# Attention and expert kernel on one Trainium2 core: other zero products in the head, six row buffers blanked later, whole sketches for the last queries, a new written order

## The chip, the core and the metric

The kernel runs on one core of a Trainium2 chip. A core has five engines that run their own instruction streams side by side and wait for one another by semaphores: TensorE (PE in the profile; its weight loads are PEld), VectorE (DVE), ScalarE (ACT), GpSimd (POOL) and SyncE (SP), which only issues transfers. The metric is the time of one execution on the device, in microseconds, as the median of the runs. The profile shows one execution; its times count from the first instruction of the span.

## The reference

```python
def phi(x):
    a = np.einsum('rd,bhsd->bhsr', S1, x)
    b = np.einsum('rd,bhsd->bhsr', S2, x)
    return np.einsum('bhsi,bhsj->bhsij', a, b).reshape(*x.shape[:-1], r * r)
q_p, k_p = (phi(q), phi(k))
kv = np.einsum('bhsf,bhsd->bhfd', k_p, v)
z = np.sum(k_p, axis=2)
num = np.einsum('bhsf,bhfd->bhsd', q_p, kv)
den = np.einsum('bhsf,bhf->bhs', q_p, z)[..., None] + 1e-06
attn = num / den                       # (4, 4, 1088, 32) -> x: 4352 rows of 128
...
e_idx = np.argmax(x @ w_gate, axis=1)  # 8 experts
...
for e in range(E):
    h = np.maximum(x[mask] @ w1[e], 0.0)          # 128 -> 1024
    out[mask] = gate_w[mask, None] * eom[mask, e, None] * (h @ w2[e])
```

Everything is in 32-bit floats. The attention is linear: keys and queries are turned into 64 products each ("sketches"), the keys' products are summed with the values for each of 4 batches, and each query's products are multiplied by these sums. Then each of the 4352 rows goes through the one expert of eight that its logits choose.

## The kernel before, in words

The program is a set of named steps, each bound to one engine, and `ORDER` is a written list of their names. The steps are emitted in that order, and every engine keeps its own steps in it. A step whose input is not there holds up all that stands behind it on its engine. The number of a step is a group of 512 rows (0 to 8; group 8 has 256), a batch (0 to 3) or a tile of 128 rows.

Attention, by groups. `Lk.g`, `Lq.g`, `Lv.g` (SP) load keys, queries and values into rings of 4, 3 and 4 buffers. `Sk.g`/`Sq.g` (PE) make the sketches, in one of two forms: a group listed in `QUARTERS` takes products of 64x64 (L400) into the ring `w`, any other takes products of 128x128, called whole (L406), into the ring `t`. Both rings lie in PSUM and have two buffers. `B` (ACT, L424) copies one half of the sketch, `M` (DVE, L429) adds the other half to it and gives the PSUM buffer back, `P` (DVE, L437) multiplies out. `A g.b` (PE, L466) sums keys times values of batch b; `C`, `KV` (ACT) copy the sums out, `GT`, `GC`, `GM`, `GK` make the gate's columns of them. `T g` (PE, L515) turns a group of query products, `TC` (ACT) copies it, `N g` (PE, L532) multiplies it by the sums, `R` (ACT, L545) copies the outcome, `X` (DVE, L557 to L562) makes the logits.

Routing, in three routes of three groups. When a route's last `X` is done, `CA`, `CB` (DVE), `PL` (PE), `WE`, `LA`, `SL`, `HP`, `HT` (DVE) give each row its place; `ST` (SP) stores the rows to DRAM (`xt`); `ID` (PE, L646) and `IA`, `IX` (DVE, L651 to L661) make the lists of row numbers.

Experts, by tiles of 128 rows. `F t` (POOL, L802) gathers a tile's rows from `xt` by the list, `XD` (DVE, L812) divides, `TN` (PE, L816) turns, `TC.t` (DVE, L822) copies, `UP` (PE, L829), `RL`, `DN` (PE, L843) and `Y` are the expert's two layers, `O` (POOL, L942) scatters the rows into the output. The first list serves tiles 0 to 7 and needs `IX0` and `ST0`; tiles 0 to 15 go alone, later tiles in groups of three (L881 to L922). `W e a` (ACT's queue, L228) loads half of an expert's weights, 512 KB.

Head. Before anything is loaded, PE runs products of zeros (`zeros`, L167): `WARM` of them at first, and one and two behind the two small products that turn the sketch matrices (`turn_rows`, L318). ACT blanks the sums' buffers and all 12 row buffers `xin` (`blank`, L369) before its first `B`.

Of the kernel before, what the change touches and what calls it, by code (L numbers as in the profile page):

```python
# [34 lines left out]
ORDER = """
Lk.0 Lk.1 Lk.2 Lk.3 Sk.0 Bk.0 Mk.0 Pk.0 Lq.0 Lq.1 Lv.0 Lv.1 Lv.2 Lq.2 Sk.1 Bk.1 Sk.2 Sq.1 A0.0 Sq.0 Bq.1 Bk.2 Mk.1 Pk.1 Mq.1 Mk.2 Pk.2 Bq.0 A1.0 A2.0
Lk.4 Lq.3 LG Lq.4 Sq.2 Bq.2 Lk.5 Lv.3 Lk.6 Lq.5 Lv.4 Sk.3 Mq.0 Pq.1 Pq.0 Mq.2 KV0 Bk.3 C0 WG Mk.3 Pk.3 T1 Sq.4 GT0 T0 Bq.4 GC0 Sk.4 Mq.4 Pq.4 GM0 CF0
A2.1 CC0 TC0 Bk.4 W00 GK0 N0 Mk.4 Pk.4 Pq.2 A3.1 A4.1 Sq.3 TC1 R0 C1 GT1 GC1 Bq.3 X0 KV1 T2 Sk.6 Mq.3 Pq.3 GM1 N1 Lq.6 Lk.7 Lv.5 Lv.6 Lk.8 CF1 TC2 W01
Bk.6 W10 GK1 Mk.6 Pk.6 N2 R1 R2 A4.2 Sq.5 Sk.5 T4 T3 X1 X2 CA0 Bk.5 Bq.5 Mq.5 TC4 CB0 Mk.5 Pk.5 TC3 Sk.7 Sq.6 Bq.6 CE0 N3 PL0 Bk.7 R3 Mq.6 WE0 LA0 SL0
HP0 HT0 Lv.7 Lv.8 Lq.7 Lq.8 ST0 A5.2 A6.2 C2 GT2 KV2 GC2 GM2 Sq.7 GK2 N4 R4 Pq.5 ID0 CF2 IA0 IX0 Mk.7 Pk.7 LC F0 F1 F2 A6.3 Sk.8 T5 Bk.8 Bq.7 Mk.8  # L40
Pk.8 CN0 A7.3 A8.3 TC5 Sq.8 W11 Bq.8 C3 Mq.7 Pq.7 N5 XD0 Mq.8 CT0 TN0 T7 TC.0 XD1 GT3 TN1 R5 TC7 W20 W21 GC3 X3 TC.1 X4 XD2 Pq.8 UP0 UP1 RL0 W30 W31
W40 RL1 TN2 DN0 GM3 T8 Y0 W41 CC1 GK3 KV3 TC8 DN1 X5 CA1 TC.2 CB1 PL1 CN1 F3 F4 F5 F6 O0 XD3 Pq.6 F7 CE1 CT1 CF3 KD N8 N7 TN3 R8 UP2 Y1 R7 W50 W51 RL2
W60 XD5 TC.3 XD4 WE1 LA1 SL1 HP1 TN4 UP3 RL3 TN5 TC.5 XD6 T6 TC.4 HT1 DN2 TC6 TN6 N6 R6 ST1 ID1 UP4 DN3 TC.6 IA1 IX1 X6 XD7 X7 X8 CA2 W61 RL4 CC2 CB2
W70 Y2 UP5 DN4 TN7 TC.7 UP6 Y3 RL5 W71 O1 O2 O3 F8 F9 F10 F11 F12 Y4 RL6 CN2 PL2 SL2 XD8 DN5 UP7 TN8 CE2 WE2 HP2 TC.8 XD9 LA2 HT2 DN6 TN9 TC.9 XD11
XD10 EN RL7 Y5 Y6 UP8 RL8 TN11 TN10 DN7 Y7 DN8 Y8 UP9 TC.10 UP10 TA XD12 O4 F13 TC.11 XD13 FT1 ID2 RL9 ST2 FW45 FW41 FW43 DN9 Y9 ZY TN12 O5 F14 IA2
IX2 O6 F15 F16 O7 F17 TC.12 UP11 RL10 DN10 Y10 RL11 DN11 Y11 TN13 UP12 F18 F19 F20 O8 F21 O9 F22 O10 F23 XD15 TC.13 XD14 UP13 TN14 RL12 TN15 DN12
TC.14 UP14 RL13 FT0 XG0 TC.15 DN13 FT2 NG0 UP15 RL14 Y12 Y13 DN14 Y14 XG1 RL15 DN15 Y15 CG0 O11 F24 O12 F25 O13 F26 O14 F27 FW44 FW42 FW40 NG1 UA0
RG0.0 RG0.1 CG1 UB0 RG0.2 RG0.3 XG2 O15 F28 F29 F30 DG0 UA1 YC0 RG1.0 RG1.1 BG0 NG2 CG2 YG0 UB1 RG1.2 RG1.3 F31 O16 F32 O17 F33 O18 XG3 DG1 UA2 YC1
RG2.0 RG2.1 BG1 NG3 CG3 YG1 UB2 RG2.2 RG2.3 F34 O19 F35 O20 F36 O21 XG4 DG2 UA3 YC2 RG3.0 RG3.1 BG2 NG4 CG4 YG2 UB3 RG3.2 RG3.3 F37 O22 F38 O23 F39
O24 XG5 DG3 UA4 YC3 RG4.0 RG4.1 BG3 NG5 NT CG5 FI FX YG3 UB4 RG4.2 RG4.3 F40 O25 F41 O26 F42 O27 XG6 DG4 UA5 YC4 RG5.0 RG5.1 BG4 NG6 CG6 YG4 UB5 RG5.2  # L50
RG5.3 F43 O28 F44 O29 O30 DR30 XG7 DG5 UA6 YC5 RG6.0 RG6.1 BG5 NG7 CG7 YG5 UB6 RG6.2 RG6.3 O31 O32 O33 XD40 XD41 DG6 UA7 YC6 RG7.0 RG7.1 BG6 TN40
TC.40 YG6 XD42 EX UB7 RG7.2 RG7.3 O34 O35 O36 DG7 YC7 TN41 TC.41 TN42 TC.42
""".split()
# [27 lines left out]
def kernel(  # L81
# [1116 lines left out]
```

## Time and profile before

| | |
|---|---|
| runs | 198.92 us median of 3 (198.47 to 199.83) |
| profiled execution | 198.53 us, span 196.5 us (2.0 us lie around the span) |
| TensorE busy | 188.5 us, 96% of the span |
| VectorE / ScalarE / GpSimd busy | 114.1 / 73.0 / 91.0 us |
| mean granted clock of TensorE | 0.977 |

Busy TensorE means that a product is under way, at whichever of its two clocks (1.2 and 2.4 GHz). Whether it could go faster has to be read from the length of equal groups at different places, and from what stands just before a gap.

### The profile page before, as it was taken

To read this page: it belongs to the slowest core of one execution; us is meant where nothing else is said; L and a number is where in the kernel's file an instruction comes from. 1 tells how busy PE (TensorE), PEld (TensorE's weight loads), DVE (VectorE), ACT (ScalarE), POOL (GpSimd) and SP (SyncE) were. 2 spreads that over 40 slices of the span, in tenths; PEclk is the share of its full clock that TensorE was granted. 3 is DMA by queue.
4 is the path that set the end of the run, shared out by engine and by line. 5 is a ranking of instruction groups with operands and counts; after the bars stand their busy time and mean duration, and the time that the engine had idled before them with its cause. 6 is when DMAs were issued, how large, how long until landed. Compare 5 with 4: busy or idle time off the path is not lost.

```text
span 196.5 us, 5598 instructions
## 1 busy us (share of the span) xinstructions
PE 188.5 (96%) x2209; PEld 170.6 (87%) x2209; DVE 114.1 (58%) x296; ACT 73.0 (37%) x173; POOL 91.0 (46%) x119
## 2 busy tenths in 40 slices
PE   7999989889999999999999999999999999999990
PEld 6999989789999999999999997777998876698990
DVE  5589869998686967568452842342633616065120
ACT  7526776643567634333022314030332221123210
POOL 1840000007726005787047877757677376235172
PEclk9999999966999999999999999999999999999997
DMA  5969965161699799456999422122112020000011
GB/s 167 344 189 314 278 240 176 59 196 46 211 326 343 219 344 292 152 177 180 414 420 403 169 59 64 52 56 63 51 30 63 3 65 14 18 17 30 27 32 30
DMA packets 14878, 31.11 MB, mean 158 GB/s; under 512 B 2553, under 2 KB 7815, under 8 KB 14064
## 3 DMA queue, kind: packets, MB, share of 16 engines
q1 hardware_dynamic: 9328, 16.44, 24.4%
q10 hardware_dynamic: 2320, 8.39, 12.7%
q0 software_dynamic: 3184, 5.65, 9.6%
q8 instruction: 31, 0.51, 1.1%
q14 instruction: 15, 0.12, 0.2%
HBM read 25.53 MB, written 5.90 MB: 160 GB/s over the span
## 4 chain that ended last, share of the span: by engine, by line
PE 46%; DMA 36%; issue 7%; POOL 5%; DVE 1%; ACT 1%; POOLq 1%; DVEq 0%; ACTq 0%
DMA xin<-xt,putf 14%; DMA out_dram<-ys,putf 14%; PE w L829 12%; DMA xin<-xt,putfar 8%; PE y L843 7%; PE t L406 6%; PE acc L843 5%; PE w L532 4%; PE acc L466 4%; POOL xin L802 3%; PE w L515 3%; POOL out_dram L942 2%; PE w L400 2%; PE t L646 1%; PE t L816 1%
## 5 line engine op out<-in xcount | busy, mean ns | idle before, releaser
L802 POOL DMA_INDIRECT xin<-xt,putf x36 | 40.7, 1131 | 50.4 <-DVE ab L429 32.6
L942 POOL DMA_INDIRECT out_dram<-ys,putf x36 | 36.2, 1006 | 41.7 <-ACT ys L846 12.1
L895 PE MATMUL w<-vt,wt 128*128 128x256 f32 (+5 forms) x128 | 32.3, 396 | 0.0
L829 PE MATMUL w<-xsT,wt 128*128 128x128 f32 x256 | 30.8, 276 | 0.0
L829 PEld LDWEIGHTS w<-xsT,wt 128*128 128x128 f32 x256 | 29.7, 192 | 0.1
L895 PEld LDWEIGHTS w<-vt,wt 128*128 128x128 f32 x128 | 22.7, 190 | 6.0 <-DVE kT L901 0.4
L901 DVE TENSOR_SCALAR kT<-w 128x768 f32<-128x768 f32 x8 | 7.7, 957 | 32.9 <-PE w L895 32.9
L834 ACT ACTIVATE hT<-w 128x1024 f32<-128x1024 f32 x13 | 13.3, 1023 | 19.6 <-PE w L829 19.6
L843 PE MATMUL y<-wt,hT 128*128 128x128 f32 x144 | 17.7, 276 | 0.0
L843 PEld LDWEIGHTS y<-wt,hT 128*128 128x128 f32 x144 | 16.8, 192 | 0.1
L912 PE MATMUL acc<-kT,wt 128*128 128x256 f32 (+5 forms) x64 | 16.2, 396 | 0.1
L912 PE MATMUL acc<-qT,wt 128*128 128x256 f32 (+5 forms) x64 | 16.0, 392 | 0.0
L916 ACT COPY kT<-acc 128x384 f32<-128x384 f32 x8 | 3.8, 478 | 30.9 <-PE acc L912 30.9
L912 PEld LDWEIGHTS acc<-kT,wt 128*128 128x128 f32 x64 | 11.7, 190 | 3.6 <-issue 0.6
L912 PEld LDWEIGHTS acc<-qT,wt 128*128 128x128 f32 x64 | 11.8, 190 | 2.9
L843 PE MATMUL acc<-wt,hT 128*128 128x128 f32 x112 | 13.7, 275 | 0.0
L843 PEld LDWEIGHTS acc<-wt,hT 128*128 128x128 f32 x112 | 13.1, 192 | 0.0
L903 ACT ACTIVATE qT<-w 128x768 f32<-128x768 f32 x8 | 6.5, 810 | 13.9 <-PE w L895 13.9
L466 PE MATMUL acc<-vt,kp 128*64 128x33 f32 (+1 forms) x288 | 11.2, 230 | 0.0
L532 PE MATMUL w<-kz,qpT 64*64 64x49 f32 x544 | 10.6, 227 | 0.5 <-issue 0.5
L437 DVE TENSOR_TENSOR kp<-ab 128x1024 f32<-128x1024 f32 (+1 forms) x9 | 10.5, 1166 | 0.7 <-PE acc L466 0.3
L466 PEld LDWEIGHTS acc<-vt,kp 128*64 128x64 f32 (+1 forms) x288 | 10.1, 144 | 0.7
(184 smaller groups left out, 297.3 us busy)
## 6 DMA issues: line engine op xcount, KB each, us to landing
wt<-in_w_dram ACTq DMA_DIRECT2D x16, 512.0 KB, 6.0
xall<-in_w_dram SPq DMA_DIRECT2D x3, 1024.0 KB, 9.9
xt<-xall SPq DMA_DIRECT2D x2, 1176.0 KB, 6.5
vt<-in_v_dram SPq DMA_DIRECT2D x8, 260.0 KB, 5.3
kT<-in_k_dram SPq DMA_DIRECT2D x8, 256.0 KB, 3.9
qT<-in_q_dram SPq DMA_DIRECT2D x8, 256.0 KB, 3.8
qp<-in_w_dram SPq DMA_DIRECT2D x1, 1024.0 KB
qpT<-in_w_dram SPq DMA_DIRECT2D x1, 1024.0 KB, 14.2
```

What stands on the lines that cost most here:

```text
L406: nc.tensor.matmul(ps[:, j].rearrange("p i x -> p (i x)"), src[:, j * 128:(j + 1) * 128], Sb.rearrange("p i h x -> p (i h x)"), start=True ...
L437: nc.vector.tensor_mul(res[:, :n], bview(av, [list(av.ap[1]), list(av.ap[2]), [0, r]]), bview(bv, [list(bv.ap[1]), [0, r], list(bv.ap[2])]))
L466: nc.tensor.matmul(now["acc", b][64 * h:64 * (h + 1), s], kp[p0:p0 + n, heads_at("k", g, j, s) + h].rearrange("s i j -> s (i j)"), now["v" ...
L532: nc.tensor.matmul(ps[64 * t:64 * (t + 1), h, 2 * j + s], now["qT", g][64 * h:64 * (h + 1), 2 * j + s, 64 * t:64 * (t + 1)], kz[(c * 128 + ...
L802: nc.gpsimd.indirect_dma_start(out=xin[room(t)], out_offset=None, in_=xt[:n, :], in_offset=bass.IndirectOffsetOnAxis(ap=index(t), axis=0), ...
L829: nc.tensor.matmul(ps[:, c], w[:, c], x[:, own(t)], start=True, stop=True)
L834: nc.scalar.activation(out, now["h", t], ACTF.Relu)
L843: nc.tensor.matmul(ps, h[:, c], w[:, c], start=(c == 0), stop=(c == FC - 1))
L895: nc.tensor.matmul(now["h", "g", e, s][:, c, :n], w[:, s * (FC // 4) + c], x[:, :n], start=True, stop=True)
L901: nc.vector.tensor_scalar_max(wide_h[s], src, 0.0)
L912: nc.tensor.matmul(ps[:, :n], w[:, c], wide_h[c // (FC // 4)][:, c % (FC // 4), :n], start=(c == 0), stop=(c == FC - 1))
L942: apart("out", nc.gpsimd.indirect_dma_start(out=out, out_offset=bass.IndirectOffsetOnAxis(ap=index(t), axis=0), in_=at_ys(t), in_offset=No ...
```

## The change

Four things. The zeros of the head become one product of 512 columns and one of 256 (before, five of 128), then one of 128 behind the first turned matrix (before, one of 64) and one of 192 behind the second (before, two of 48). Six of the 12 row buffers are blanked in two new steps of ScalarE, `BX0` and `BX1`, which stand in the order behind `Bk.1` and behind `R2`. The query groups 6, 7 and 8 leave `QUARTERS`, so that their sketches are whole. And the written order is a new one, up to the start of the grouped tiles; from there on it is the old one.

```diff
-WARM = 5
+WARM = (4, 2)
-QUARTERS = {("k", 0), ("q", 0), ("k", 1), ("q", 6), ("q", 7), ("q", 8)}
+QUARTERS = {("k", 0), ("q", 0), ("k", 1)}
 ORDER = """
-Lk.0 Lk.1 Lk.2 Lk.3 Sk.0 Bk.0 Mk.0 Pk.0 Lq.0 Lq.1 Lv.0 Lv.1 Lv.2 Lq.2 Sk.1 Bk.1 Sk.2 Sq.1 A0.0 Sq.0 Bq.1 Bk.2 Mk.1 Pk.1 Mq.1 Mk.2 Pk.2 Bq.0 A1.0 A2.0
+Lk.0 Lk.1 Lk.2 Lq.0 Lq.1 LG Lv.0 Lv.1 Sk.0 Bk.0 Mk.0 Pk.0 Lk.3 Lk.4 Lq.2 Sk.2 Sk.1 Sq.0 Bk.2 Bk.1 BX0 A0.0 Mk.2 Pk.2 Mk.1 Pk.1 Sq.1 Bq.1 Bq.0 Sq.2
...
-    def zeros(n, w=128):
-        for i in range(n):
-            nc.tensor.matmul(warm[:, 0, :w], idle, idle[:, :w], start=True, stop=True)
-    zeros(WARM)
+    def zeros(n, k, w):
+        for _ in range(n):
+            nc.tensor.matmul(warm[:, 0, :k * w].rearrange("p (k x) -> p k x", x=w), idle, bview(idle, [[0, k], [1, w]]), start=True, stop=True)
+    for k in WARM:
+        zeros(1, k, DM)
...
-        zeros(1 + i, 64 - 16 * i)
+        zeros(1, 1 + i, 128 - 32 * i)
...
-    for t in xin:
+    at_first = len(xin) - 6
+    for t in xin[:at_first]:
         blank(t, 2, W // 2)
+
+    def blank_rows(i):
+        for t in xin[at_first + 3 * i:at_first + 3 * (i + 1)]:
+            blank(t, 2, W // 2)
...
+    for i in range(2):
+        add(f"BX{i}", "ACT", [], lambda i=i: blank_rows(i))
```

What the new order moves stands in the engines' own rows. First VectorE of the kernel before, from the query products of group 5 to the first tile's division; `rows_of` to `putf` are `IA0` and `IX0`, which finish the first list, and `xdiv` is `XD0`:

```order
L437 TENSOR_TENSOR qp<-ab_226 128x1024
L651 COPY rows_of<-t_64 128x80
L659 TENSOR_TENSOR valf_902<-rows_of 128x8
L660 TENSOR_SCALAR nonef_903<-valf_902 128x8
L661 SCALAR_TENSOR_TENSOR putf_904<-valf_902,nonef_903 128x8
L429 TENSOR_TENSOR ab_225<-t_65,ab_225 128x256
L437 TENSOR_TENSOR kp<-ab_225 128x1024
L429 TENSOR_TENSOR ab_226<-t_64,ab_226 128x128
L437 TENSOR_TENSOR kp<-ab_226 128x512
L429 TENSOR_TENSOR ab_225<-w_66,ab_225 128x256
L437 TENSOR_TENSOR qp<-ab_225 128x1024
L812 TENSOR_TENSOR xdiv_262<-xin 128x128
```

The same stretch of the changed kernel, from the list on, where lines stand six higher:

```order
L657 COPY rows_of<-t_64 128x80
L665 TENSOR_TENSOR valf_927<-rows_of 128x8
L666 TENSOR_SCALAR nonef_928<-valf_927 128x8
L667 SCALAR_TENSOR_TENSOR putf_929<-valf_927,nonef_928 128x8
L443 TENSOR_TENSOR qp<-ab_216 128x1024
L435 TENSOR_TENSOR ab_217<-t_65,ab_217 128x256
L563 RECIPROCAL xall<-xall 128x16
L565 TENSOR_TENSOR lg_225<-xall 128x256
L567 TENSOR_TENSOR lg_225<-lg_225 128x4x32
L568 TENSOR_TENSOR L_227<-lg_225 128x64
L443 TENSOR_TENSOR qp<-ab_217 128x1024
L818 TENSOR_TENSOR xdiv_252<-xin 128x128
```

The key products of groups 7 and 8 (`kp`) stood behind the list and now stand ahead of it; behind it come the queries of groups 7 and 6 and the logits of group 3.

TensorE of the kernel before, from the sketch of query group 8 to the first up products (L829, tiles 0 and 1) and a little behind them:

```order
L400 MATMUL w_67<-Sb,qT 64x64 x8
L532 MATMUL w_66<-kz_207,qpT 64x49 x32
L816 MATMUL t_64<-ident,xdiv_262 128x128
L515 MATMUL w_67<-ident,qp 128x128 x8
L490 MATMUL t_65<-ident,kv_233 64x128
L816 MATMUL t_64<-ident,xdiv_263 128x128
L829 MATMUL w_66<-xsT_260,wt_92 128x128 x8
L829 MATMUL w_67<-xsT_260,wt_94 128x128 x8
L816 MATMUL t_65<-ident,xdiv_262 128x128
L843 MATMUL y_69<-wt_93,hT 128x128 x8
L501 MATMUL t_64<-wgb,kzT_231 64x32 x2
```

The same stretch of the changed kernel:

```order
L412 MATMUL t_64<-Sb,qT 128x128 x2
L521 MATMUL w_67<-ident,qp 128x128 x8
L538 MATMUL w_66<-kz_203,qpT 64x49 x32
L538 MATMUL w_67<-kz_204,qpT 64x49 x32
L698 MATMUL t_65<-cum_240,ones 64x8 x2
L822 MATMUL t_64<-ident,xdiv_252 128x128
L521 MATMUL w_66<-ident,qp 128x128 x8
L822 MATMUL t_64<-ident,xdiv_253 128x128
L835 MATMUL w_67<-xsT_250,wt_89 128x128 x8
L835 MATMUL w_66<-xsT_250,wt_91 128x128 x8
L521 MATMUL w_67<-ident,qp 128x128 x4
L849 MATMUL y_69<-wt_90,hT 128x128 x8
```

`N7` (the second row of 64x49) and `T6` (the second L521) have come ahead of the first up products, and the sketch of query group 8 is two whole products in the place of eight small ones. `GM3` (L501) has moved far ahead as well.

ScalarE of the changed kernel, where the sums of batch 1 are kept (`KV1`, the four rows of `kz`) and query group 3 is copied (`Bq.3`, the row of `ab`):

```order
L513 COPY kz_201<-t_64 64x2x16 x2
L488 COPY kz_202<-acc_68 64x2x32
L489 COPY kz_202<-acc_68 64x2
L488 COPY kz_202<-acc_68 64x2x32
L489 COPY kz_202<-acc_68 64x2
L591 COPY oh_237<-carry 128x8
L430 COPY ab_217<-t_65 128x256
```

In the kernel before `Bq.3` stood ahead of `KV1`; now it stands behind it.

## Rows read from the trace of the kernel before

**Rows 1.** The page: busy time of each engine, and the granted clock in 40 slices.

```profile
PE 188.5 (96%) x2209; PEld 170.6 (87%) x2209; DVE 114.1 (58%) x296; ACT 73.0 (37%) x173; POOL 91.0 (46%) x119
PEclk9999999966999999999999999999999999999997
```

**Rows 2.** Stretches: start:end, length, busy us (instructions) by engine, clock, DMA share, GB/s.

```profile
35.00:40.00 5.00, 3.92 (x155) 3.40 (x147) 4.76 (x13) 3.48 (x15) 0.00 (x0) 1.00 0.32 100
40.00:45.00 5.00, 5.00 (x138) 4.66 (x139) 4.57 (x10) 1.53 (x5) 0.03 (x1) 0.58 0.48 147
45.00:50.00 5.00, 5.00 (x121) 4.63 (x123) 3.42 (x7) 1.88 (x5) 4.08 (x4) 0.74 0.33 99
190.00:196.50 6.50, 1.65 (x15) 1.46 (x14) 0.35 (x1) 0.27 (x1) 2.67 (x3) 0.84 0.11 33
```

**Rows 3.** All waits of PE: us in total, times, longest.

```profile
PE w L167 <- DVE maskh L231: 1.1, 1, 1.1
PE t L501 <- ACT kzT L494: 0.6, 1, 0.6
PE w L532 <- issue: 0.5, 1, 0.5
PE t L490 <- ACT kv L476: 0.5, 1, 0.5
```

**Rows 4.** The chain that ended last, 43.9 to 55.9 us: start, us, what.

```profile
43.89 0.18 DVE putf L661
44.97 0.33 POOL xin L802
...
47.07 4.41 DMA xin<-xt,putf
51.50 0.30 DVE xdiv L812
51.85 0.33 PE t L816
52.18 3.72 PE w L829 x32
```

**Rows 5.** Time line of PE: start, us, what. The head, then equal groups at full clock.

```profile
1.14 2.50 PE L167 MATMUL w<-ys 128*128 128x128 f32 x10 [1.14 <-DVE maskh L231]
4.86 1.09 PE L167 MATMUL w<-ys 128*128 128x48 f32 x4
5.88 1.99 PE L400 MATMUL w<-Sb,kT 64*64 64x64 f32 x64
7.79 2.07 PE L406 MATMUL t<-Sb,kT 128*128 128x128 f32 x8
16.70 1.06 PE L406 MATMUL t<-Sb,qT 128*128 128x128 f32 x8
21.82 1.36 PE L466 MATMUL acc<-vt,kp 128*64 128x33 f32 x40
34.67 0.70 PE L400 MATMUL w<-Sb,qT 64*64 64x64 f32 x32
```

**Rows 6.** The same time line: groups at 44 to 71 us.

```profile
45.60 1.91 PE L515 MATMUL w<-ident,qp 128*128 128x128 f32 x8
57.72 0.30 PE L501 MATMUL t<-wgb,kzT 64*64 64x32 f32 x4
60.88 1.87 PE L532 MATMUL w<-kz,qpT 64*64 64x49 f32 x96
66.64 1.04 PE L515 MATMUL w<-ident,qp 128*128 128x128 f32 x8
```

**Rows 7.** Time line of ACT: blanks and the first copies of sketches.

```profile
3.76 3.17 ACT L369 COPY xin<-ys 128x196 f32<-128x196 f32 x12
7.08 0.37 ACT L424 COPY ab<-w 128x256 f32<-128x256 f32 x1 [0.15 <-PE w L400]
10.95 0.65 ACT L424 COPY ab<-t 128x256 f32<-128x256 f32 x2 [2.65 <-PE t L406]
```

**Rows 8.** Waits of DVE from 7 to 45 us.

```profile
DVE ab L429 <- ACT ab L424: 3.6, 4, 2.3
DVE xall L557 <- ACT xall L546: 1.0, 1, 1.0
```

**Rows 9.** Time line of DVE: the key products of groups 7 and 8.

```profile
44.42 1.22 DVE L437 TENSOR_TENSOR kp<-ab 128x1024 f32<-128x1024 f32 x1
46.15 0.29 DVE L429 TENSOR_TENSOR ab<-t,ab 128x128 f32<-128x128 f32 x1 [0.50 <-ACT ab L424]
```

More of the change, by code (lines that the diff above doesn't have):

```diff
@@ L33 @@
 NY = 6
-QUARTERS = {("k", 0), ("q", 0), ("k", 1), ("q", 6), ("q", 7), ("q", 8)}
+QUARTERS = {("k", 0), ("q", 0), ("k", 1)}
 ORDER = """
-Lk.0 Lk.1 Lk.2 Lk.3 Sk.0 Bk.0 Mk.0 Pk.0 Lq.0 Lq.1 Lv.0 Lv.1 Lv.2 Lq.2 Sk.1 Bk.1 Sk.2 Sq.1 A0.0 Sq.0 Bq.1 Bk.2 Mk.1 Pk.1 Mq.1 Mk.2 Pk.2 Bq.0 A1.0 A2.0
-Lk.4 Lq.3 LG Lq.4 Sq.2 Bq.2 Lk.5 Lv.3 Lk.6 Lq.5 Lv.4 Sk.3 Mq.0 Pq.1 Pq.0 Mq.2 KV0 Bk.3 C0 WG Mk.3 Pk.3 T1 Sq.4 GT0 T0 Bq.4 GC0 Sk.4 Mq.4 Pq.4 GM0 CF0
-A2.1 CC0 TC0 Bk.4 W00 GK0 N0 Mk.4 Pk.4 Pq.2 A3.1 A4.1 Sq.3 TC1 R0 C1 GT1 GC1 Bq.3 X0 KV1 T2 Sk.6 Mq.3 Pq.3 GM1 N1 Lq.6 Lk.7 Lv.5 Lv.6 Lk.8 CF1 TC2 W01
@@ L39 @@
[L39 to L50, printed above, removed]
@@ L51 @@
-RG5.3 F43 O28 F44 O29 O30 DR30 XG7 DG5 UA6 YC5 RG6.0 RG6.1 BG5 NG7 CG7 YG5 UB6 RG6.2 RG6.3 O31 O32 O33 XD40 XD41 DG6 UA7 YC6 RG7.0 RG7.1 BG6 TN40
-TC.40 YG6 XD42 EX UB7 RG7.2 RG7.3 O34 O35 O36 DG7 YC7 TN41 TC.41 TN42 TC.42
+Lk.0 Lk.1 Lk.2 Lq.0 Lq.1 LG Lv.0 Lv.1 Sk.0 Bk.0 Mk.0 Pk.0 Lk.3 Lk.4 Lq.2 Sk.2 Sk.1 Sq.0 Bk.2 Bk.1 BX0 A0.0 Mk.2 Pk.2 Mk.1 Pk.1 Sq.1 Bq.1 Bq.0 Sq.2
+Bq.2 Mq.1 Mq.0 Pq.1 Mq.2 Pq.0 A1.0 Lk.5 Lv.2 Lv.3 A2.0 Lq.3 Lv.4 Lk.6 Lq.4 Lq.5 Sk.4 Sk.5 T1 W00 C0 Bk.4 Bk.5 KV0 Mk.4 WG Mk.5 Pk.4 Sk.3 CF0 A2.1 Bk.3
@@ new lines @@
+W01 TC1 Pq.2 Mk.3 Pk.3 T0 GT0 Sq.3 GC0 TC0 W10 GM0 A3.1 A4.1 GK0 N0 KV1 CC0 Bq.3 R0 Sk.6 Bk.6 C1 Pk.5 Mq.3 Pq.3 Mk.6 X0 T2 Sq.4 GT1 Bq.4 GC1 TC2 N1
+GM1 CF1 A4.2 Lk.7 Lv.5 Lv.6 Lq.6 Lq.7 Lk.8 Lv.7 Lv.8 Mq.4 Pq.4 Pk.6 GK1 N2 A5.2 Sk.7 Sk.8 A6.2 W11 R1 R2 BX1 Bk.8 Bk.7 KV2 W20 W21 C2 T4 X1 X2 CA0
+Mk.8 Mk.7 Pk.7 CB0 Sq.5 CF2 A6.3 Bq.5 TC4 CE0 Mq.5 Pk.8 A7.3 GT2 GC2 PL0 A8.3 GM2 C3 GK2 WE0 LA0 SL0 HT0 HP0 T3 GT3 Sq.7 GC3 GM3 TC3 Bq.7 GK3 N4 KV3
+R4 Sq.6 Mq.7 ID0 Pq.5 N3 IA0 IX0 ST0 Lq.8 LC F0 F1 F2 F3 F4 T5 Sq.8 W30 Bq.6 R3 Pq.7 T7 TC5 Bq.8 TC7 W31 N5 R5 Mq.6 X3 Pq.6 XD0 Mq.8 Pq.8 N7 CF3 KD
@@ new lines @@
+CN0 TN0 T6 TC.0 XD1 TN1 CT0 TC.1 R7 CC1 TC6 UP0 UP1 RL0 W40 T8 RL1 DN0 X4 X5 CA1 XD3 XD2 CB1 PL1 SL1 CN1 CT1 N6 CE1 Y0 TC8 W41 N8 R6 W50 W51 TN3 TN2
+DN1 TC.2 TC.3 XD4 UP2 TN4 F5 F6 HT1 XD5 O0 F7 Y1 R8 CC2 RL2 W60 TN5 UP3 WE1 LA1 TC.4 UP4 ST1 X6 DN2 HP1 X7 XD6 TC.5 XD7 X8 CA2 RL3 DN3 TN6 ID1 IA1 IX1
+TC.6 RL4 W61 Y2 W70 Y3 W71 UP5 TN7 CB2 TC.7 CE2 WE2 UP6 CN2 PL2 DN4 RL5 DN5 RL6 Y4 DN6 Y5 Y6 O1 O2 O3 F8 F9 F10 F11 F12 O4 F13 O5 F14 O6 SL2 HP2 HT2
+XD8 TN8 XD9 TC.8 UP7 RL7 EN XD10 TN9 ID2 IA2 XD11 TC.9 LA2 IX2 TA ST2 FW40 UP8 TN10 UP9 TN11 RL8 DN7 Y7 TC.11 TC.10 XD13 RL9 XD12 TN13 DN8 Y8 DN9 Y9
@@ new lines @@
+TN12 TC.12 UP10 RL10 UP11 UP12 XD14 FT2 DN10 Y10 F15 F16 O7 F17 F18 F19 RL11 TC.13 TN14 DN11 Y11 RL12 ZY FT1 UP13 RL13 TC.14 XD15 XG0 DN12 DN13 NG0
+FT0 TN15 TC.15 Y12 UP14 UP15 RL14 Y13 DN14 RL15 DN15 FW42 FW44 F20 O8 CG0 Y14 F21 XG1 O9 Y15 F22 O10 F23 O11 F24 O12 F25 O13 F26 O14 F27 FW45 FW41
+FW43 UA0 RG0.0 NG1 CG1 RG0.1 UB0 RG0.2 RG0.3 XG2 O15 F28 F29 F30 DG0 UA1 YC0 RG1.0 RG1.1 BG0 NG2 CG2 YG0 UB1 RG1.2 RG1.3 F31 O16 F32 O17 F33 O18 XG3
+DG1 UA2 YC1 RG2.0 RG2.1 BG1 NG3 CG3 YG1 UB2 RG2.2 RG2.3 F34 O19 F35 O20 F36 O21 XG4 DG2 UA3 YC2 RG3.0 RG3.1 BG2 NG4 CG4 YG2 UB3 RG3.2 RG3.3 F37 O22
@@ L53 @@
+F38 O23 F39 O24 XG5 DG3 UA4 YC3 RG4.0 RG4.1 BG3 NG5 NT CG5 FI FX YG3 UB4 RG4.2 RG4.3 F40 O25 F41 O26 F42 O27 XG6 DG4 UA5 YC4 RG5.0 RG5.1 BG4 NG6 CG6
+YG4 UB5 RG5.2 RG5.3 F43 O28 F44 O29 O30 DR30 XG7 DG5 UA6 YC5 RG6.0 RG6.1 BG5 NG7 CG7 YG5 UB6 RG6.2 RG6.3 O31 O32 O33 XD40 XD41 DG6 UA7 YC6 RG7.0 RG7.1
+BG6 TN40 TC.40 YG6 XD42 EX UB7 RG7.2 RG7.3 O34 O35 O36 DG7 YC7 TN41 TC.41 TN42 TC.42
 """.split()
```

## The prediction

> **What bounds the kernel now.** I read the page first: TensorE is busy for 188.5 of 196.5 us, no other engine for more than 60% [rows 1]. Its list of waits is short: 1.1 us at the start, and three waits of half a microsecond [rows 3]; the end costs 4.9 us more, since of the last 6.5 us it works in 1.65 [rows 2]. So the time is TensorE's work, and what a change can win is of three kinds: waits, stretches at the lower clock, and work that goes away.
>
> Then the stretches. The granted clock is 0.58 in 40 to 45 us and 0.74 in 45 to 50 [rows 2]. With two levels, 1.2 and 2.4 GHz, a mean of 0.58 is 4.2 us at the lower one and 0.74 is 2.6, together 6.8 us. Just before the fall TensorE had waited for ScalarE twice, 0.5 and 0.6 us [rows 3], and was busy for only 3.92 us of 5 [rows 2]. What it costs shows on equal groups: eight turns take 1.91 us at 45.60 and 1.04 at 66.64 [rows 6]. The head is slow too, though the clock column does not say so: eight whole sketch products take 2.07 us at 7.79 and 1.06 at 16.70 [rows 5].
>
> Last the chain. From 43.9 to 52 us it does not run through TensorE: the first list (`putf`) is ready at 44.07, the first gather starts at 44.97, the second at 47.07 and lands 4.41 us later, `XD1` and `TN1` follow at 51.50 and 51.85, and the up products at 52.05 to 52.18 [rows 4]. So the first up product stands **8.0 us behind the list**, whatever TensorE does meanwhile; the work between is filler. This decides the case: what TensorE loses ahead of 52 us has been paid partly by filler that was there anyway.
>
> **The change part by part.**
>
> *Zeros.* Ten passes of 128 columns took 2.50 us, about 0.22 each [rows 5]. By columns, 512 and 256 take six times 128 in each of two passes, 12 x 0.213 = 2.56 us against 10 x 0.213 = 2.13: 0.4 us more, which makes the first turned matrix about 0.2 us later (PE had a 0.2 us hole there). The last zeros fall from four passes (1.0 us, as long for 48 columns as for 128 [rows 5]) to two of 0.32: 0.4 us less. So the first sketch starts 0.2 us earlier, at about 5.7. The denser head may also bring the full clock before the 8 to 10 us at which it came. That is worth at most 1.0 us in the group at 7.79 [rows 5] and the same again in the small sketches ahead of it (1.99 us for 64 passes against twice 0.5), but VectorE is next there: it needs 1.6 us for every group it adds and multiplies (0.41 + 1.22 [rows 9]) and then has no hole. I take 0.3 us from VectorE's earlier start, with 0 and 1.0 as ends.
>
> The Trainium skill ("TensorE: Matmul & The Clock Gate", section "What's actually happening") says that the number of slow products at the start differs from run to run and that the ramp is less than 1% of a typical span and nothing to fit to. The rows agree with the size: the slow head costs about 2 us of TensorE. By that rule the head would give nothing that can be counted on, a rival below.
>
> *Blanks.* Twelve take 3.17 us, 0.26 each [rows 7]. Six fewer free ScalarE 1.6 us earlier, but its first copy had waited for TensorE already (0.15 us [rows 7]): nothing. `BX0` and `BX1`, 0.8 us each, fall into holes of ScalarE such as the 2.65 us ahead of 10.95 [rows 7]. If a hole is gone, 0.8.
>
> *Whole sketches.* A quartered group of 32 passes takes 0.52 us from start to start (0.70 with its tail), a whole one 0.89 (1.06) [rows 5]: 0.37 more for groups 6 and 7, half as much for group 8, together 0.9 us of TensorE. All three stand ahead of the first up product, where TensorE waits. Cost 0; 0.9 if that cover is gone.
>
> *The order, behind the first up product.* Three pieces have moved from behind it to ahead of it: `N7`, two thirds of 1.87 us = 1.25; `T6`, 0.87 (1.04 less the tail); `GM3`, 0.23 [rows 6]. TensorE works without a wait from there to 191.6 us, so the end comes **2.35 us earlier** if the first up product stays where it is. In the later part, the second list and third list stand at about the same number of tiles or earlier; I find no new wait there, and the grouped tiles are untouched.
>
> *The order, ahead of it.* The first list needs VectorE. It now does the keys of groups 7 and 8 first: 1.6 and 0.9 us [rows 9], so 2.5 us later. Against that go VectorE's waits up to the list: 1.0 for the logits of group 1, and 3.6 for copies less the 2.3 before its first instruction, 1.3 [rows 8], about 0.5 in smaller ones; with the 0.3 of the earlier start, 3.1 less. One wait is new. `Mq.3` needs `Bq.3`, which stands on ScalarE behind `KV1`; `KV1` waits for the sums `A3.1` and `A4.1`, 1.3 us of TensorE [rows 5] that start only when `Pk.3` is done. Behind `Pk.3` VectorE has one product (1.1 us) to do, while sums, tail, keeping (0.55), and the copy (0.37) take 2.7: it waits 1.6 us, with all products of groups 3 to 8, and so the list, behind it. Sum: 2.5 - 3.1 + 1.6 = **1.0 us later**, list at 45.1, first up product at 53.0. Ends: 0.5 earlier (no such wait) and 2.5 later.
>
> *Sum.* 2.35 - 1.0 = 1.35 us. The profiled execution took 198.53, which gives 197.2; the median of the runs is 0.4 above it, which gives 197.6. I forecast 197.4.
>
> The dip at 40 to 50 us adds nothing to this, which is the step most easily got wrong. Its 3.4 us, and the two waits ahead of it, were filler time: without them TensorE runs out of filler earlier. Before, it arrived at `TN1` with about 0.1 us to spare. Now it saves 3.4 us of dip, 1.6 of waits and some of the head, about 6, gets 2.35 + 0.9 us more to do, and so waits about 2 us in front of `TN1` and another 1 to 2 on the way.
>
> **The rivals.**
>
> *A. That wait brings the clock down again.* Two microseconds of nothing, with one small turn within, are more than the 1.1 us of waits after which the clock fell before [rows 3]. Then the first up products run at 1.2 GHz, and behind them nothing is filler any more: what they lose, the end loses. The old dip, 6.8 us long, would have cost 3.4; dense up products should bring the clock back sooner, so I take half, 1.7: 199.1. For it: the length of the wait. Against it: the fall before came among small products (33 columns), and here whole turns and up products stand on both sides.
>
> *B. The clock falls earlier, and the list is late: slower.* Between 33 and 42 us VectorE leads, and TensorE has the sums `A6.3` to `A8.3` (33 columns) between short waits, the mixture that stood before the fall at 41. At 1.2 GHz the three whole sketches and turns ahead of `ID0` take 1 us more each [rows 6]; VectorE has about 1 us to spare there, so from a fall ahead of 40 us the list comes 2 to 2.5 us later still, and the first up product with it: 199.9; with A behind it, 201.6. It decides from 2.35 us of delay on.
>
> *C. The list is not late.* If ScalarE's copies cost VectorE nothing, the list comes 0.5 us earlier than before, and the end at 196.0.
>
> *D. The head does nothing.* The clock rises no earlier; then the second sketch, now a whole one, takes 2.07 us [rows 5] and VectorE waits for copies about 1 us more: 198.4. This is what the skill's sentence on the ramp comes to here.
>
> **How the numbers follow.** Forecast 0.35 (196.6 to 198.2), A 0.25 (198.2 to 200), B 0.15 (199 to 201.6), C 0.15 (195 to 196.9), D 0.10 (198 to 198.8). What a measurement of this kernel can tell from no change is about 1%: under 196.9 and over 200.9. Faster by that: C, some of the forecast's lower part, 0.33. Slower: a part of B and little of A, 0.13. The rest, 0.54, is within 1%. The range 195.6 to 200.2 leaves out the ends of C and B.
>
> **What would show it.** Right: the list (`putf`) at 44.5 to 46 us, first up product 8 us behind it, a wait of TensorE of 1 to 2 us in front of `TN1`, a wait of VectorE of about 1.6 us at 22 us behind `Pk.5`, no wait of TensorE behind the first up product, and no stretch of 6.8 us at the lower clock. Wrong: the gathers land much sooner than 8 us behind the list, or TensorE gets to `TN1` after its rows are there (then dips and the 0.9 us of whole sketches count in full), or the clock is low in 50 to 57 us.

## Result and the profile after

The changed kernel took 199.69 us (median of 20 runs), the kernel before 198.2 beside it; the ratio is **1.0058, interval 1.003 to 1.0085**. The ratio leaves out the slow runs of both kernels (five of the 20 of the changed one, one of them of 315.43 us), so it is not the quotient of the two medians. The forecast was 197.4, 0.8% under the 198.92 of before; the changed kernel is about 0.6% slower, by an interval that excludes 1, though inside the 1% that counts as no change.

The profiled execution took 198.44 us, with the same span as before. The page of the changed kernel; rows 1 to 3 answer to [rows 1], the last is TensorE's code, 29 packets of some 16 KB:

```profile
span 196.5 us, 5459 instructions
PE 186.1 (95%) x2141; PEld 166.3 (85%) x2141; DVE 113.7 (58%) x296; ACT 72.9 (37%) x173; POOL 89.7 (46%) x119
PEclk9999999999999999999999999999999999999999
q8 instruction: 29, 0.48, 0.9%
```

The dip at 40 to 50 us is gone and TensorE does 2.4 us less busy time, yet the span is the same. TensorE's waits, the longest groups (us in total, times, longest), to set against [rows 3]:

```profile
PE acc L849 <- issue: 1.6, 1, 1.6
PE w L167 <- DVE maskh L232: 1.1, 1, 1.1
...
PE w L901 <- DVE kT L907: 0.5, 1, 0.5
...
PE t L822 <- DVE xdiv L818: 0.4, 1, 0.4
PE w L538 <- issue: 0.4, 1, 0.4
PE t L652 <- DVE ab L435: 0.2, 1, 0.2
```

A wait of 1.6 us that no other engine releases heads the list. First the part that came out near the forecast, VectorE and TensorE up to the first up product (start, length, operation, wait ahead of it in brackets); it answers to [rows 4]. From 20.14 on the rows are `Pk.3`, `Pk.5`, `Mq.3` and the end of the first list:

```profile
16.12 0.42 DVE L435 TENSOR_TENSOR ab<-t,ab 128x256 f32<-128x256 f32 x1 [1.12 <-ACT ab L430]
...
20.14 1.23 DVE L443 TENSOR_TENSOR kp<-ab 128x1024 f32<-128x1024 f32 x1
22.88 1.22 DVE L443 TENSOR_TENSOR kp<-ab 128x1024 f32<-128x1024 f32 x1 [1.51 <-PE acc L472]
24.37 0.42 DVE L435 TENSOR_TENSOR ab<-t,ab 128x256 f32<-128x256 f32 x1 [0.27 <-ACT ab L430]
...
45.53 0.17 DVE L667 SCALAR_TENSOR_TENSOR putf<-valf,nonef 128x8 int32<-128x8 f32 x1
...
52.27 0.29 DVE L818 TENSOR_TENSOR xdiv<-xin 128x128 f32<-128x128 f32 x1 [0.72 <-DMA xin<-xt,putf]
```

```profile
49.46 1.27 PE L538 MATMUL w<-kz,qpT 64*64 64x49 f32 x70 [0.36 <-issue]
50.67 0.29 PE L698 MATMUL t<-cum,ones 128*64 128x8 f32 x4
50.89 0.33 PE L822 MATMUL t<-ident,xdiv 128*128 128x128 f32 x1
51.10 1.09 PE L521 MATMUL w<-ident,qp 128*128 128x128 f32 x8
52.62 0.33 PE L822 MATMUL t<-ident,xdiv 128*128 128x128 f32 x1 [0.42 <-DVE xdiv L818]
```

List at 45.70 (forecast 45.1), first up product at 52.79 (53.0). The new wait of VectorE has the forecast size (1.51 us and 0.27, forecast 1.6), but most of it stands elsewhere: not behind `Pk.5`, for the copy `Bq.3`, but ahead of `Pk.5`, for sums of TensorE (L472), which give back one of the two `kp` buffers. Then the end. The last two rows of before, TensorE at 187.91 and 189.70, and those of the changed kernel:

```profile
187.91 1.95 PE L843 MATMUL acc<-kp,hT 128*128 128x128 f32 x16
189.70 1.95 PE L843 MATMUL y<-qp,hT 128*128 128x128 f32 x16
```

```profile
186.42 1.95 PE L849 MATMUL y<-kp,hT 128*128 128x128 f32 x16
190.01 2.02 PE L849 MATMUL acc<-qp,hT 128*128 128x128 f32 x16 [1.64 <-issue]
```

The last product but one starts 1.49 us earlier than before: the forecast gain, 1.35, had arrived. Then TensorE stands still for 1.64 us, and the last product starts 0.31 later than before. In that time TensorE's own queue (PEldq) is in the branch that leaves the chain of last tiles (its `If` for tile 2 turns out false, and the last down product stands in the `Else`). First the branch of before, then that of the changed kernel (duration in ns, minimum/median/maximum, then its start):

```profile
L1130 PEldq COMPARE_BRANCH  x1: 1085/1085/1085, 187.7 to 187.7; - x1
```

```profile
L1138 PEldq COMPARE_BRANCH  x1: 3620/3620/3620, 186.2 to 186.2; - x1
```

Before, 1.09 us lay hidden behind products already queued. Now 3.62 us don't. No line of the diff touches this place.

### The profile page after: what moved, and what is told of

Its sections match the earlier page's. It is cut to its first block, busy times and chain, and to the rows that moved or that the text cites. A ratio compares the mean times of both kernels' runs of the same rounds, so it can differ in the third digit from the quotient of the medians.

```text
span 196.5 us, 5459 instructions
## 1 busy us (share of the span) xinstructions
PE 186.1 (95%) x2141; PEld 166.3 (85%) x2141; DVE 113.7 (58%) x296; ACT 72.9 (37%) x173; POOL 89.7 (46%) x119
## 4 chain that ended last, share of the span: by engine, by line
DMA 50%; PE 22%; issue 10%; DVE 10%; POOL 4%; ACT 1%; SPq 1%; POOLq 1%; DVEq 0%; ACTq 0%
DMA out_dram<-ys,putf 19%; DMA xin<-xt,putf 15%; DMA xin<-xt,putfar 8%; PE w L835 7%; PE y L849 4%; DMA xt<-xall 3%; DMA vt<-in_v_dram 3%; PE acc L849 3%; DMA qT<-in_q_dram 2%; POOL xin L808 2%; PE t L412 2%; POOL out_dram L948 2%; PE w L538 1%; PE acc L472 1%; DVE qp L443 1%
## 5 line engine op out<-in xcount | busy, mean ns | idle before, releaser
L808 POOL DMA_INDIRECT xin<-xt,putf x36 | 38.5, 1070 | 47.9 <-ACT xall L551 34.5
L901 PE MATMUL w<-vt,wt 128*128 128x256 f32 (+5 forms) x128 | 32.5, 396 | 0.5 <-DVE kT L907 0.5
L901 PEld LDWEIGHTS w<-vt,wt 128*128 128x128 f32 x128 | 22.7, 190 | 6.3 <-DVE kT L907 1.0
L907 DVE TENSOR_SCALAR kT<-w 128x768 f32<-128x768 f32 x8 | 7.6, 956 | 27.9 <-PE w L901 27.9
L918 PE MATMUL y<-kT,wt 128*128 128x256 f32 (+5 forms) x64 | 16.1, 395 | 0.0
L918 PE MATMUL y<-qT,wt 128*128 128x256 f32 (+5 forms) x64 | 16.0, 392 | 0.0
L849 PE MATMUL y<-wt,hT 128*128 128x128 f32 x128 | 15.7, 276 | 0.0
L849 PE MATMUL acc<-wt,hT 128*128 128x128 f32 x128 | 15.7, 276 | 0.0
L922 ACT COPY kT<-y 128x384 f32<-128x384 f32 x8 | 3.8, 478 | 31.1 <-PE y L918 31.1
L849 PEld LDWEIGHTS y<-wt,hT 128*128 128x128 f32 x128 | 14.9, 192 | 0.1
L918 PEld LDWEIGHTS y<-kT,wt 128*128 128x128 f32 x64 | 11.6, 190 | 3.2 <-issue 0.2
L918 PEld LDWEIGHTS y<-qT,wt 128*128 128x128 f32 x64 | 11.8, 190 | 2.9
L472 PE MATMUL acc<-vt,kp 128*64 128x33 f32 (+1 forms) x288 | 10.9, 224 | 1.1 <-DMA vt<-in_v_dram 0.6
L909 ACT ACTIVATE qT<-w 128x768 f32<-128x768 f32 x8 | 6.5, 810 | 14.3 <-PE w L901 14.3
L472 PEld LDWEIGHTS acc<-vt,kp 128*64 128x64 f32 (+1 forms) x288 | 9.6, 137 | 2.2 <-DMA vt<-in_v_dram 0.7
L907 DVE TENSOR_SCALAR qT<-w 128x768 f32<-128x768 f32 x8 | 7.7, 958 | 5.5 <-PE w L901 5.4
```

The lines of the kernel that those rows point to most:

```text
L472: nc.tensor.matmul(now["acc", b][64 * h:64 * (h + 1), s], kp[p0:p0 + n, heads_at("k", g, j, s) + h].rearrange("s i j -> s (i j)"), now["v" ...
L808: nc.gpsimd.indirect_dma_start(out=xin[room(t)], out_offset=None, in_=xt[:n, :], in_offset=bass.IndirectOffsetOnAxis(ap=index(t), axis=0), ...
L849: nc.tensor.matmul(ps, h[:, c], w[:, c], start=(c == 0), stop=(c == FC - 1))
L901: nc.tensor.matmul(now["h", "g", e, s][:, c, :n], w[:, s * (FC // 4) + c], x[:, :n], start=True, stop=True)
L907: nc.vector.tensor_scalar_max(wide_h[s], src, 0.0)
L909: nc.scalar.activation(wide_h[s], src, ACTF.Relu)
```

## Experiments

Ten of the kernels ran on two chips where every kernel, that of before too, took 211 to 232 us, with holes in TensorE's stream; of those ten (`after_again`, `before_again`, `after_old_seam`, `after_old_zeros`, `after_dead16`, `after_dead136`, `before_dead120`, `before_new_zeros`, `after_long_first`, `after_long_last`) only the trace is used. Places are counted in TensorE's compiled program.

**Repeats, the old seam, the old zeros.** `after_again` and `before_again` are the two kernels unchanged. `after_old_seam` puts the pieces at the start of the grouped tiles in another order, since a wait of 0.49 us stands there (L901); `after_old_zeros` takes back the zeros alone.

> The changed kernel with the four steps at the start of the grouped tiles as in the kernel before (NG1 ahead of UA0, RG0.1 ahead of CG1). Theory 1 says that the 0.5 us wait of TensorE in the first group's up products comes from VectorE's RG0.1, which stands behind CG1 and so behind NG1: the wait goes and the time is 0.4 to 0.5 us (0.2%) below the changed kernel's. Rival: the wait has another cause (the ring of two PSUM buffers), stays, and the time is the same.

> The changed kernel with the zero products of the kernel before. Theory (my prediction's term): the clock rises later (at about 10 us and not at 5), VectorE's first products come up to 1 us later, the list and the first up product with them, and the time is 0.3 to 1.0 us longer. Rival (the head is covered): the list is late by less than 0.3 us and the time is within 0.2% of the changed kernel's.

```diff
-UA0 RG0.0 NG1 CG1 RG0.1 UB0          (after_old_seam)
+NG1 UA0 RG0.0 RG0.1 CG1 UB0
```

The seam's wait stayed and only changed its releaser:

```profile
138.51 1.80 PE L901 MATMUL w<-vt,wt 128*128 128x304 f32 x6 [0.51 <-ACT kT L909]
```

So it doesn't come from this order, and is not where 1.5 us went. Both releasers (L907, L909) are the steps that empty a buffer of the ring `w` and give it back, which speaks for the ring as the cause; no run changes the ring. The long branch came back in `after_again` (4.18 us, gap 2.19) and `after_old_seam` (3.67, gap 1.68), and not in `before_again` (1.30, none). With the old zeros it was 2.04, without a gap. Their only mark on that place is four more small products, 16 instructions, ahead of it. Hence the suspicion that the place of the code counts.

**Shifting the whole program.** The same zero columns in more or fewer products.

```diff
-WARM = (4, 2)
+WARM = (2, 2, 1, 1)      (after_split8;  after_split16: (1,) * 6)
-WARM = 5                 (before_merge8, with the new zeros() and the old counts behind it)
+WARM = (2, 2, 1)
```

> The changed kernel with its first 768 columns of zeros as products of 256, 256, 128 and 128 columns and not of 512 and 256: the same columns, two products more, which puts every later instruction of TensorE 8 places on (each such product is four instructions), to the place in a stretch of 128 at which the kernel before has its last branch. Theory C: the branch takes 1.1 to 1.3 us as in the kernel before, no gap ahead of the last down product, which begins some 1.6 us earlier than in the changed kernel (188.4 on the first chip against 190.0); time 0.992 of the changed kernel, and 0.997 of the kernel before. Theory T: the gap of 1.6 us stays, and the time is that of the changed kernel within 0.3%. A head theory (shorter zeros let TensorE's clock rise later) would show the granted clock low for longer in the first 10 us and the first up product 1 us later; not expected, since the columns are the same.

> The same with six zero products of 128 columns: 16 places on, where the run with the old zeros had a branch of 2.04 us. Theory C: a branch of about 2.0 us, a gap under 0.4 us ahead of the last down product, time 0.993 to 0.995 of the changed kernel. Theory T: the gap of 1.6 us stays and the time is that of the changed kernel within 0.3%.

> The kernel before with its 640 columns of zeros as products of 256, 256 and 128 and not as five of 128: the same columns, two products fewer, so every later instruction of TensorE stands 8 places earlier, where the changed kernel has its last branch. Nothing else is changed. Theory C: the branch takes 3.6 us or more, the last down product of the kernel before begins about 1.6 us late (191.3 on the first chip against 189.7), time 1.006 to 1.010 of the kernel before. Theory T: the branch takes 1.1 to 1.3 us as before, no gap, and the time is that of the kernel before within 0.3%.

`after_third`, unchanged, stood beside them: branch 4.19, gap 2.21. `after_split8` kept 3.49 us and a gap of 1.51; ratio to before 1.0065 (1.0013 to 1.0118). `after_split16`: 1.65, no gap, **0.9944 (0.9903 to 0.9985)**. `before_merge8`: 1.06, no gap, 0.9995 (0.9963 to 1.0028). So the place may count, but not as expected: 8 instructions did not suffice for the one and did not harm the other. Places within stretches of 128 are out.

**Target or origin?** Products written where no run enters shift code without executing anything. In the body of the last of 32 tiles they move only the ways out.

```diff
             up(t)
+            if k == NL - 1:
+                for _ in range(4):     (after_dead136: 34; before_dead120: 30)
+                    nc.tensor.matmul(now["h", t][:, 0], weights(t)[0][:, 0], xsTs[t // 2 % 2][:, own(t)], start=True, stop=True)
```

> The changed kernel, with four more products written into the body of the last of the 32 tiles, which no run of this input enters: nothing more is executed, the branch stands where it stood, and only what lies behind that body, the 32 ways out among it, is 16 instructions further on. Target theory (the branch out of the chain takes long because its target's code is loaded then, and how long depends on where the target lies): the branch takes 1.6 to 2.0 us as in the runs with six zero products and with the old zeros, whose way out lay at the same place; the gap ahead of the last down product goes from 1.64 us to under 0.3, and the time is 0.992 to 0.995 of the changed kernel, 0.997 to 0.999 of the one before. Origin theory (it depends on where the branch itself lies): 3.6 us and a gap of 1.6 us stay, and so does the time of the changed kernel. Zeros theory (six short zero products did it, by what they do in the head): likewise no change.

> The same with 34 such products: the way out lies within one instruction of where it lies in the kernel before (10728 instructions into TensorE's program, there 10729), the branch still where the changed kernel has it. Target theory: the branch takes 1.1 to 1.3 us, no gap, the last down product begins at 188.3 to 188.5 us where the first chip's numbers hold, time 0.992 of the changed kernel and 0.997 to 0.999 of the one before. Origin theory: 3.6 us and a gap of 1.6 us stay.

> The kernel before with 30 products in the body of the last tile, which is not entered: its way out moves from 10729 to 10849 instructions into the program, 257 behind that of the changed kernel, and nothing else moves. If the place counts within stretches of 256 instructions, the branch takes 3.5 us or more, and the last down product begins 1.5 us late: time 1.007 of the kernel before. If the place counts otherwise (within 128, or by the branch's own place), 1.1 us, no gap, and the time is that of the kernel before within 0.3%.

The target theory fell: `after_dead16` 3.98 us and a gap of 2.00, `after_dead136` (target where before has it) 3.57 and 1.59, `before_dead120` 0.68 and none.

```profile
209.85 1.95 PE L849 MATMUL y<-kp,hT 128*128 128x128 f32 x16
213.79 3.51 PE L849 MATMUL acc<-qp,hT 128*128 128x128 f32 x15 [2.00 <-issue]
```

**Moving the branch.** The same trick in a case of the last expert's group down product that its width doesn't take moves the branch and everything behind it.

```diff
         def columns(n):
             for c in range(FC):
                 ...
+            if e == E - 1 and n == WIDTHS[-1]:
+                for _ in range(4):     (after_shift128: 32; before_shift120: 30)
+                    nc.tensor.matmul(ps[:, :TS], w[:, 0], wide_h[0][:, 0, :TS], start=True, stop=True)
```

> The changed kernel with 32 more products written into the last expert's group down product, in the case for widths over 336, which that expert doesn't take: nothing more is executed, and the branch out of the chain and its target both move 128 instructions on, the branch to 7544, between the places 7537 and 7553 at which it was short in the kernels before. Origin theory (the branch's own place decides how long the load of its target holds it): 1.1 to 1.3 us, no gap, the last down product begins 1.6 us earlier, time 0.992 of the changed kernel and 0.994 to 0.999 of the one before. Head theory (what differs is something the head's products do, not the place): 3.6 us or more, the gap of 1.6 to 2.2 us stays, time of the changed kernel within 0.3%.

> The same with 4 such products: the branch at 7432, where the runs with the old zeros and with six zero products had 2.04 and 1.65 us. Origin theory: 1.6 to 2.1 us, a gap under 0.3 us, time 0.993 to 0.995 of the changed kernel. Head theory: 3.6 us or more and the gap stays.

> The kernel before with 30 such products: the branch at 7673, 257 behind that of the changed kernel. If the place counts within stretches of 256 instructions: a branch of 3.5 us or more and a gap of about 1.6 us ahead of the last down product, time 1.007 of the kernel before. If it counts within 128 or not in this way: 1.1 us, no gap, the time of the kernel before within 0.3%.

The origin theory held in all three as to the gap, though not every size that it gave. `after_shift16` has the whole gain and no gap, span 195.0:

```profile
186.35 1.95 PE L849 MATMUL y<-kp,hT 128*128 128x128 f32 x16
188.13 1.95 PE L849 MATMUL acc<-qp,hT 128*128 128x128 f32 x16
```

```profile
L1141 PEldq COMPARE_BRANCH  x1: 1672/1672/1672, 186.1 to 186.1; - x1
```

and `before_shift120`, the kernel before with padding, gets the gap, though it executes the same products as ever:

```profile
181.50 1.34 PE L912 MATMUL acc<-kT,wt 128*128 128x256 f32 x5 [1.15 <-issue]
...
189.17 1.95 PE L843 MATMUL acc<-kp,hT 128*128 128x128 f32 x16
192.46 2.02 PE L843 MATMUL y<-qp,hT 128*128 128x128 f32 x16 [1.34 <-issue]
```

Its ratio is 1.0166 (1.0099 to 1.0233), more than the 1.007 expected: a second hole of 1.15 us came at the group product whose dispatch now jumps over the padding. `after_shift16` has **0.9948 (0.9906 to 0.999)**; `after_fourth`, the changed kernel beside it, 1.0003 (0.9944 to 1.0063), branch 3.88, gap 1.89. These two intervals overlap, so the gain of the shift rests on the trace as much as on the times; and the 0.6% that the changed kernel lost on the first chip was not seen again on this one, though its interval allows it.

`after_shift128` lost its gap (branch 2.01, 1.1 to 1.3 expected), but its time, 1.0004 (0.9962 to 1.0046), shows no gain: in its profile the second gather landed 5.43 us after its issue (3.99 in the changed kernel) and the last scatter 3.92 (2.16). Whether these belong to it or to that one execution stays open. Between them it has the whole gain: from the first up product to the last down product it takes 135.8 us, `after_shift16` 135.4 and `after_split16` 135.7, against 137.2 to 138.3 in after, `after_third`, `after_fourth` and `after_split8`, which have the gap, and 137.65 in before.

Not all of a gap reaches the end. From TensorE's last product to the end of the span it is 4.4 us in those four traces, 5.0 in `after_shift16` and 4.7 in `after_split16`: in `after_shift16` the last scatter is issued 1.4 us behind the one ahead of it (3.2 in after) and lands 2.69 us after its issue (2.16). There TensorE's last product ends 1.94 us earlier than in after, and the span is 1.4 shorter.

What the branch waits for can be read from the packets of TensorE's code queue (q8). Place is the branch's, modulo 256; the packet is the last one that landed ahead of the branch's end.

| kernel | place | branch us | its packet begins, against the branch | branch ends behind the packet |
|---|---|---|---|---|
| after, _again, _third, _fourth, _old_seam, _dead16, _dead136 | 248 | 3.57 to 4.19 | 1.01 to 1.66 later | 1.33 to 1.50 |
| before_shift120 | 249 | 3.33 | 1.03 later | 1.34 |
| after_split8 | 0 | 3.49 | 1.01 later | 1.39 |
| after_old_zeros, _split16, _shift16, _long_first, _long_last | 8 | 1.65 to 2.10 | 0.42 to 0.69 earlier | 1.42 to 1.50 |
| before_new_zeros, before_merge8, after_shift128 | 113 to 121 | 1.06 to 2.01 | 0.30 to 1.52 earlier | 1.36 to 1.38 |
| before, before_again, before_dead120 | 129 | 0.68 to 1.30 | 1.20 to 1.63 earlier | 1.36 to 1.38 |

In all 20 traces the branch ends 1.3 to 1.5 us behind the landing of a packet of code. A hint (`BRANCH_PREFETCH_HINT`) that names the branch stands 2.9 us ahead of it in every trace. Where the branch lies at the end of a stretch of 256 (or on its edge), the packet begins only 1.0 us or more after the branch itself; elsewhere it has begun 0.3 to 1.6 us ahead of it. With the packet's own time and the 1.3 to 1.5 us behind it, that accounts for the difference in the branch's length. The place alone doesn't decide whether time is lost: the next branch of TensorE's queue took 2.60 to 3.44 us in six traces, that of before among them (2.67), but no product stands behind it. The Trainium skill ("Runtime: NRT & Kernel Launch", section "Instruction fetch mechanics") says that code comes in blocks of 256 instructions, fetched in sequence, and that a taken branch out of the window forces a fetch. The traces agree: TensorE's code comes in 29 to 31 packets of some 16 KB, and the branch ends 1.3 to 1.5 us behind one of them. That the hint's load has to wait for the next block in sequence is my reading; no run shows the reason. The hint moves with the branch in every shift, so the runs don't tell whether its place or the branch's counts, and only the places in the table were tried.

**The head.** `before_new_zeros` is the kernel before with the four new zero products alone.

> The kernel before with the four new zero products alone (512, 256, 128 and 192 columns); order, blanks and quarter sketches as they were. The forecast gave the head as a whole 0.3 us, of it nearly all by TensorE's clock being full from 5 us of the span on and not from 10. Theory H (the head's products wait for loads and copies, so the earlier clock gives little): the first sketch earlier by 0 to 0.3 us, the first up product at 52.0 as in the kernel before or up to 0.4 us earlier, time 0.998 to 1.000 of the kernel before. Rival (the earlier clock carries through): the first up product 1 us earlier, time 0.995. The way out lies at 10713, 8 instructions ahead of where the kernel before with merged zeros had it: 1.1 us and no gap if the target theory is right.

Its trace shows no gain: first sketch at 6.08 (5.88 before), list at 44.14 (43.16 to 44.87 in the other traces of before), first up product at 51.99. But the traces beside each other show two heads with the new zeros, and this one has the slower (64 sketch passes in 1.99 us, as before), so it doesn't tell what the faster one would give. The changed kernel's first profile, and then `after_fourth`, the same program:

```profile
5.62 0.69 PE L406 MATMUL w<-Sb,kT 64*64 64x64 f32 x32
6.27 1.16 PE L412 MATMUL t<-Sb,kT 128*128 128x128 f32 x8
```

```profile
6.09 1.13 PE L406 MATMUL w<-Sb,kT 64*64 64x64 f32 x32
7.20 2.08 PE L412 MATMUL t<-Sb,kT 128*128 128x128 f32 x8
```

With the first form (after, `_again`, `_third`, `_old_seam`, `_shift16`, `_shift128`) the list is ready at 45.2 to 45.8; `after_split16` has it too, but waited for loads. With the second (`_fourth`, `_split8`, `_dead16`, `_dead136`) it is ready at 46.5 to 47.7, and the first up product of `after_fourth` starts at 54.82 in place of 52.79. All six traces with the old zeros (merged or not) have slow passes there, and `after_old_zeros` its list at 48.04, where `after_again` and `after_old_seam` on the same chip have 45.22 and 45.32: later by 2.7 us, where up to 1 was expected. Two runs asked whether more zeros bring the first form; both ran on one of the two chips named above, so that only their traces count.

```diff
-WARM = (4, 2)                          (after_long_first)
+WARM = (4, 3)
-        zeros(1, 1 + i, 128 - 32 * i)  (after_long_last)
+        zeros(1, 1 + 2 * i, 128)
```

> after_shift16 with 384 columns in the second zero product of the head and not 256. Theory R (whether the early form of the head comes depends on TensorE having had enough zeros without a hole): 0.4 us more of zeros, the first turned matrix at most 0.4 us later, and the early form (32 sketch passes in 0.69 us) in nearly all runs, so that the runs no longer fall into two groups 1 to 2 us apart: time 0.990 to 0.993 of the kernel before. Theory N (the form is by chance, whatever the zeros): two groups as with after_shift16, each 0.2 to 0.4 us later, time 0.995 to 0.998.

> after_shift16 with 384 columns in the last zero product, behind the second turned matrix, and not 192: 0.16 to 0.32 us more, which ends at about 5.9 us and then stands ahead of the first sketch. Theory R: the early form in nearly all runs, time 0.990 to 0.994 of the kernel before. Theory N: two groups, time 0.995 to 0.998.

`after_long_first` had the first form, `after_long_last` the second (first sketch at 6.73). So length alone doesn't settle it; what does stays open. The granted clock is 1.00 from 0 to 10 us in the windows of both forms, so the row of the clock doesn't tell them apart; the passes' durations do.

## Why the prediction was wrong

- **"TensorE works without a wait from there to 191.6 us"**: the step that failed. The 2.35 us of work moved ahead measured 2.23 (first up product to last but one down product: 135.86 us before, 133.63 after). I read the end of before as free of waits and took it to stay so. Its exit branch was 1.09 us, hidden behind queued products, and its packet had begun 1.32 us ahead of it; the change shortened TensorE's program by 137 instructions and put the branch on place 248 of a stretch of 256. In every trace of this layout that costs TensorE a wait of 1.6 to 2.2 us, more than the 1.35 forecast. With the branch 16 instructions on, the change measures 0.9944 and 0.9948, which of 198.92 is 197.8 to 197.9, against 197.4 forecast.
- **What stays open**: in the profiled execution the wait only undoes the gain, and the span is that of before. Why the 20 runs are 0.6% slower and not equal isn't shown. The head (below) may be a reason; the form of the other 19 runs isn't known. The median, 199.69, lies in the ranges of rivals A and B, but no fall of the clock, the cause of both, shows in the trace.
- **List 1.0 us later**: 1.65 in the first profile. From VectorE's first sum of sketches (6.79, 7.48 before) to the list its work grew by 1.85 us, not by 2.5, and its start came 0.7 earlier, not 0.3. Most mis-sized were the old waits that were to go: 2.8 by the forecast, 1.3 measured (one of 1.12 us for a copy stands at 16.12). The new wait was right in size (1.78 for 1.6) and mostly wrong in its cause: a buffer of `kp`, not the copy behind `KV1`. The way from list to up product was shorter than the 8.0 taken over from before: 7.09, since the second gather was issued 2.6 us behind the list (3.0 before) and landed in 3.99 (4.41). That the first up product came within 0.2 us of the forecast is luck: the two misses cancel.
- **Head 0.3 us (0 to 1.0)**: mis-sized. In the new order the list hangs on the head: by its two forms it comes at 45.2 to 45.8 or at 46.5 to 47.7. The first profile showed the good form. Rival D was right for the other form.
- **The dip costs nothing**: no run contradicts it. Of the runs of before that the ratio of `after_split16` rests on, the seven with a mean granted clock of 0.975 to 0.979 have a median of 198.1 us, the nine with 0.995 to 0.999 one of 198.5.
- **The wait in front of `TN1`**: 0.42 us in place of 1 to 2, mis-sized. Rival A, a new fall of the clock, did not come. In other traces the wait is as long as forecast or longer, by the landing of the second gather: 2.27 in `after_split8` (5.29 us from issue to landing), 2.40 in `after_shift128`.
- **Blanks and whole sketches at nothing**: no wait in the trace contradicts it; they were not run apart.
- Rivals B and C: the list was late by 1.65, under B's 2.35 and without B's cause; C, a list that is not late, fell with it.

## What to carry to other kernels

Look at the branches out of a data-dependent chain, not only at engines: here one waited for its code, and an edit far ahead of it changed how long. Compare the duration of such a branch before and after; unexecuted instructions placed ahead of it test this without touching the work, and can win the time back, as in `after_shift16`. They aren't free: the dispatch that jumps over 30 to 32 of them took 1.5 to 1.7 us (`after_shift128`, `before_shift120`). And a single profile of a kernel whose head has two forms is one draw; list the time of an early landmark (here the first list) in every trace before explaining a median.

## What the runs showed of the hardware

- The exit branch of TensorE's queue ended 1.33 to 1.50 us behind the landing of a 16 KB packet of its code in 20 of 20 traces; it was 0.68 to 2.10 us long where the packet had begun first, 3.33 to 4.19 where it had not.
- 30 products that are only jumped over opened a hole of 1.15 us at the dispatch that jumps (`before_shift120`, a branch of 1.74 us there); 32 in `after_shift128` made a branch of 1.52 us and no hole.
- On two of the chips the same kernels took some 10% longer; the way from the first list to the first up product was 13.5 to 15.2 us in eight of the ten traces taken there, against 7.0 to 8.5 elsewhere.
